# Two attention layers on one core: the P·V sum of a second half copied out by two engines, and a score bank lent to the maxima

## The chip, the cores and the metric

The kernel runs on one core of a Trainium2 chip. The metric is the device time of one execution in microseconds (us). TensorE (PE) multiplies matrices, and its results land in eight banks of 128 partitions by 512 float32 columns; VectorE (DVE) and ScalarE (ACT) read those banks. GpSimd (POOL) works on the other memory alone, and SyncE (SP) issues most transfers.

## The reference

A block is applied twice: a Fourier mixing layer and then an attention layer, each behind a layer norm and added to its input.

```python
x = A_x                                   # 1 x 2048 x 512
x = x + _A_ref(_layernorm(x), ...)        # Re(DFT_seq(DFT_hidden(x))), as matrix products
x = x + _B_ref(_layernorm(x), wq, wk, wv, wo)
x = x + _A_ref(_layernorm(x), ...)
x = x + _B_ref(_layernorm(x), wq, wk, wv, wo)

def _B_ref(x, wq, wk, wv, wo):            # 32 heads of 16; one key and one value head for all
    q = (x @ wq).reshape(B, S, H, Dh).transpose(0, 2, 1, 3)
    k = x @ wk
    v = x @ wv
    scores = einsum("bhqd,bkd->bhqk", q, k) * Dh ** -0.5
    p = softmax(scores)
    o = einsum("bhqk,bkd->bhqd", p, v)
    return o.transpose(0, 2, 1, 3).reshape(B, S, H * Dh) @ wo
```

All is float32.

## The kernel before, in words

Both layers have the same two phases. Phase A makes the Fourier mix, the queries, keys and values. Phase B, where the change lies, makes the attention.

Phase B goes over 16 tiles of 128 queries (`i`), and over 32 steps in each tile (`s_`): a tile has two halves (`hf`) of 16 heads, and a half has 16 steps, one for each chunk of 128 keys (`c`). One step does this:

- It multiplies the probabilities of two steps ago with the values: `pv`, L1137, four products for four groups of heads, added up over the 16 steps of a half in the one bank `z`. After the sixteenth step the sum is copied out of `z` to a tile `row` (L1146 or L1148); after that the next half may begin in `z`.
- It makes four score products (`score`, L1123) in four banks `x`, which are used in turn, and ScalarE takes the exponential of each (L1125).
- It makes a share of the row maxima that later tiles need. These are score products again, in three banks `y`, from which VectorE takes maxima: two whole ones (`whole`, product L450, maximum by L451) and one in two parts (`part`). The first part's product (L1070, g = 0) is followed by a copy of one element by VectorE (L1072), for which the second part's product (L1070, g = 1) waits; one maximum (L1075) then covers both.

The three kinds are interleaved in a fixed order, written as `"asMssMsb"`: a and b are the two parts, M a whole maximum, s a score. PE is strictly in this order. Where a step has two shares of maxima instead of three, another short table sets the order.

The banks of the maxima are in a list, `o.banks`, and those of the scores in a list `o.x`. A product takes the first bank of its list, and the bank goes to the list's end when its reader has been issued.

In step 17 of each tile but the first (`out_now`) the output projection of the tile before stands ahead of the step's scores: twelve products (L102 to L104) in a bank taken from `o.banks`. ScalarE copies that bank out (L1211), and it goes to the end of `o.banks`. In tiles 1 to 5 the step has two shares of maxima, in tiles 6 to 14 three. In tile 15 the maxima run out after a few steps, and the rest of the phase uses wider banks (`wide`).

The sum of a first half is completed in step 17 too (two steps behind), just ahead of the projection; the sum of a second half in step 1 of the next tile, between ordinary steps. The copies to HBM (`o_store`) and the rest of the output's way have half a tile of time.

Waits between engines are put in by the tile framework from what each instruction reads and writes. The order on each engine is the order in which the code issues.

Of the kernel before, what the change touches and what calls it, by code (L numbers as in the profile page):

```python
# [48 lines left out]
def fnet_mqa_kernel(ctx: ExitStack, tc: tile.TileContext, x_in, ct, dt_, wq, wkv, wo, out):  # L49
    nc = tc.nc  # L50
# [5 lines left out]
    def banks_as(name):  # L56
        if layout:
            layout.pop().close()
        if name:
            layout.append(ExitStack())  # L60
            layout[0].ps = layout[0].enter_context(tc.tile_pool(name=name, bufs=1, space=PSUM, reuse_waits="tile"))
# [4 lines left out]
    def f(ap):  # L66
        return ap.bitcast(F32)

    def slot(k, dtype=F32):
        return sb.tile([P, S], dtype, name=f"slot{k}")  # L70

    def half(k, dtype=F32):
        return sb.tile([P, D], dtype, name=f"row{k}")

    def bank(tag):
        if tag == "w":
            return layout[0].ps.tile([P, 1024], F32, name=tag, bufs=3)
        if tag == "v":
            return layout[0].ps.tile([P, 512], F32, name=tag, bufs=1)
        return (psz if tag == "z" else layout[0].ps).tile([P, 512], F32, name=tag, bufs={"x": 4, "y": 3, "z": 1}[tag])  # L80

    def pair():
        return [bank("x") for _ in range(2)]
# [127 lines left out]
    def make_layer(L, src, mid, dst, last):  # L211
        o = Layer()
# [836 lines left out]
        def side():  # L1049
            return min(ahead[0][3]) if ahead else 0  # L1050

        def more_max():
            whole(side())

        def part_next():
            if parts:
                return *parts.pop(), 1
            for e, (i, pr, kb) in enumerate(todo):
                if i in o.loaded | {0} and kb > 1:
                    parts.append(todo.pop(e))  # L1060
                    return *parts[0], 0
            return None
# [23 lines left out]
        def left(j, lim):  # L1086
            def n(of):
                return sum(u[0] < j or (u[0] == j and u[1] < lim) for u in of)
            return 2 * n(todo) + n(parts) + sum(len(u[3]) for u in ahead if u[0] < j or (u[0] == j and u[1] < lim))

        def share(n):
            slack = min([3 * (at - n) - left(j, lim) for j, lim, at in goals if at > n], default=99)
            if n < NSTEP:
                st["light"] = slack >= EARLY_SPARE and not st.get("light") and n >= 4
            else:
                st["light"] = slack >= SPARE and n % NSTEP == NT + 1
            return 2 if st["light"] else 3

        def done_with(i, pr):
            return all(u[:2] > (i, pr) for u in todo + parts + ahead)  # L1100

        ptiles = {}
        wide = []
# [26 lines left out]
        def pv(i, s_):  # L1130
            hf, c = divmod(s_, NT)
            if c == 0:
                acc[i, hf] = bank("z")
            a = acc[i, hf]
            pt = ptiles.pop((i, s_))
            for j in range(4):
                nc.tensor.matmul(a[32 * j:32 * j + 32, :], v1[:, c, :], pt[:, j, :], start=c == 0, stop=c == NT - 1)  # L1137
            if c == NT - 1:
                oa = half(hf)
                if last and (i, hf) == (NT - 1, 1):  # L1140
                    ob = half(0)[:, :256]
                    nc.scalar.copy(oa[:, :256], a[:, :256])
                    nc.vector.tensor_copy(ob, a[:, 256:])
                    oa = (oa, ob)
                elif wide and hf == 0:
                    nc.vector.tensor_copy(oa, a)  # L1146
                else:
                    nc.scalar.copy(oa, a)  # L1148
                acc[i, hf] = oa

        bt = {}
# [51 lines left out]
        def o_proj(i):  # L1203
            for k in range(NK):
                o_mm(k)
            o_add(i)
# [92 lines left out]
        def phase_b(nxt):  # L1299
            nonlocal woh, wol, osp  # L1300
            o.x = pair() + pair()
            o.banks = [bank("y") for _ in range(3)]
            woh = slot(4, F32R).rearrange("p (k e) -> p k e", k=NK)
            wol = slot(5, F32R).rearrange("p (k e) -> p k e", k=NK)
            def wo_load(j):
                st["wo", j] = half(4 + j)
                nc.sync.dma_start(st["wo", j], wo[:, j, :])

            behind = []
            for n in range(NT * NSTEP):  # L1310
                i, s_ = divmod(n, NSTEP)
                if len(behind) == 2:
                    pv(*behind.pop(0))
                behind.append((i, s_))
                out_now = i > 0 and s_ == NT + 1
                if out_now:
                    o_proj(i - 1)
                n_max = share(n) if todo or parts or ahead else 0
                if n_max == 0 and not wide:
                    banks_as(f"wide{L}")  # L1320
                    o.banks = [bank("v")]
                    wide.extend(bank("w") for _ in range(3))
                at = part_next() if n_max == 3 else None
                if at:
                    for k, v in zip("asMssMsb", (0, 1, 0, 3, 0, 1, 2, 1)):
                        if k == "s":
                            score(i, s_, v)
                        elif k == "M":
                            whole(v)
                        else:  # L1330
                            part(at, v)
                else:
                    g = side()
                    turns = ((g, 0), (1 - g, min(n_max, 2)), (2 + g, 0), (3 - g, n_max - 2))
                    if out_now and n_max == 2:
                        whole(g)
                        turns = ((1 - g, 0), (g, 1), (3 - g, 0), (2 + g, 0))
                    for j, m in turns:
                        score(i, s_, j)
                        for _ in range(m):  # L1340
                            more_max()
                if n in (1, 3):
                    q_half_store(12, 2 + n // 2)
                if i == 0 and 17 <= s_ <= 23 and s_ % 2:
                    q_half_store(14, s_ // 2 - 8)
                if 12 <= n < 16:
                    wo_load(n - 12)
                if n == 25:
                    osp = slot(3, F32R).rearrange("p (a h n) -> p a h n", a=2, h=2)
                if i == 0 and s_ in (16, 18, 20, 22):  # L1350
                    j = s_ // 2 - 8
                    nc.gpsimd.tensor_copy(woh[:, j, :], st["wo", j])
                    nc.gpsimd.tensor_sub(wol[:, j, :], st["wo", j], f(woh[:, j, :]))
                if i > 0:
                    for fn in out_tasks(i - 1).get(s_, ()):
                        fn()
                for j in range(2, NT):
                    if i == (j // 4 if j < 5 else j - 4 if j < 13 else j - 2):
                        at = {2: 0, 3: 12, 4: 6}.get(j, 0)
                        if s_ == at:  # L1360
                            qT_load(j)
                        if s_ == at + 4:
                            o.loaded.add(j)
                for fn in half_tasks(i).get(s_, ()):
                    fn()
                for at, j, p0, np_ in ((NT - AHEAD, i, HALF, HALF), (NSTEP - AHEAD, i + 1, 0, HALF if i >= NT - 3 else NPAIR)):
                    if j in (0, NT - 2, NT - 1) or j == i + 1 < NT:
                        for e in range(2):
                            if s_ == at - 1 + e:
                                assert done_with(j, p0 + np_ // 2 * (e + 1) - 1)  # L1370
                                max_neg_a(j, p0, np_, parts=(e,))
                        if s_ == at + 1:
                            max_neg_b(np_, nc.gpsimd)
                        if s_ == at + 2:
                            max_rows(j, p0, np_)
            if nxt is not None:
                wide.clear()
                banks_as(f"single{L + 1}")
                nxt.a_start()
            for at in behind:  # L1380
                pv(*at)
            if nxt is not None:
                o.banks = []
            return {**out_tasks(NT - 1), 12: [lambda: o_proj(NT - 1)]}
# [67 lines left out]
```

## Time and profile before

| | us |
|---|---|
| median of 3 runs (lowest, highest) | 3451.92 (3450.12, 3452.2) |
| profiled execution | 3454.01 |
| its span (first to last instruction) | 3452.2 |
| PE busy, of the span | 3423.4 (99%) |
| DVE busy | 2655.5 (77%) |
| ACT busy | 2669.4 (77%) |
| POOL busy | 936.8 (27%) |
| copies of P·V sums by ACT (L1148), 61 of 617 ns | 37.6 |
| copies of the projection by ACT (L1211), 28 of 587 ns | 16.4 |

Phase B of the first layer runs from about 620 to 1730 us of the span, that of the second from about 2335 to the end. In the first layer tile 7 begins at about 1110 us and tile 8 at about 1180. A PE share of 99% says little, since the products are pipelined and their ends are modelled; what tells more is the time from the first P·V product of a step to that of the next, which is the step's length.

### The profile page before, as it was taken

How to read it: one execution, taken by the hardware profiler on the slowest of the kernel's cores; microseconds unless marked ns; L12 is line 12 of the kernel's file. 1: busy time of each engine (PE TensorE's matmuls, PEld its weight loads, DVE VectorE, ACT ScalarE, POOL GpSimd, SP SyncE). 2: the span in 40 equal slices, each digit the busy share in tenths (PEclk: the TensorE clock that was granted, in tenths of full speed). 3: DMA queues.
4: the chain of work that ended last, by engine and by line, in shares of the span. 5: the costliest groups of instructions: out<-in, count | busy, mean ns of one | idle time of the engine just before them, and what ended most of it. 6: DMA issues, size and time to landing. Idle time of an engine off the chain costs nothing.

```text
span 3452.2 us, 68576 instructions
## 1 busy us (share of the span) xinstructions
PE 3423.4 (99%) x25532; PEld 2012.5 (58%) x25532; DVE 2655.5 (77%) x5772; ACT 2669.4 (77%) x5248; POOL 936.8 (27%) x1478
## 2 busy tenths in 40 slices
PE   8999999999999999999999999999999999999999
PEld 6888979544444444444378979894444444444443
DVE  6264766899899999999432747668989998999893
ACT  4234644899999999999932256549999999999998
POOL 4255453312222222222312354522111111111111
PEclk9999999999999999999999999999999999999999
DMA  6445252321111110111143352423111111011110
GB/s 189 150 156 190 75 168 84 86 64 33 38 36 51 35 27 24 51 35 27 42 141 116 124 173 101 152 73 91 48 39 36 51 36 38 23 36 39 32 30 26
DMA packets 225555, 255.89 MB, mean 74 GB/s; under 512 B 52896, under 2 KB 175040, under 8 KB 218052
## 3 DMA queue, kind: packets, MB, share of 16 engines
q1 hardware_dynamic: 210932, 234.04, 22.0%
q0 software_dynamic: 14144, 17.33, 1.6%
q8 instruction: 201, 3.29, 0.4%
q14 instruction: 134, 1.10, 0.1%
q10 hardware_dynamic: 144, 0.13, 0.0%
HBM read 187.69 MB, written 65.79 MB: 73 GB/s over the span
## 4 chain that ended last, share of the span: by engine, by line
PE 92%; issue 3%; POOL 2%; ACT 1%; DVE 1%; DMA 0%; DVEq 0%; SPq 0%; ACTq 0%; POOLq 0%
PE z L1137 30%; PE x L1123 13%; PE x L893 11%; PE y L1070 10%; PE y L450 8%; PE y L102 3%; PE y L541 3%; PE y L103 2%; PE y L104 2%; PE x L102 2%; PE x L104 2%; PE x L103 2%; PE z L541 1%; PE w L1115 1%; PE z L289 1%
## 5 line engine op out<-in xcount | busy, mean ns | idle before, releaser
L1125 ACT ACTIVATE slot<-x 128x512 f32<-128x512 f32 x3904 | 1994.7, 609 | 27.2 <-PE x L1123 7.3
L451 DVE TENSOR_REDUCE mxp<-y 128x1 f32<-128x512 f32 x1956 | 1259.9, 685 | 89.9 <-PE x L1123 24.7
L1137 PE MATMUL z<-slot,v 128*32 128x512 f32 x8192 | 1102.6, 605 | 0.0
L1123 PE MATMUL x<-slot,kz 64*128 64x512 f32 x2880 | 805.0, 427 | 0.3 <-DMA slot<-craw 0.2
L1075 DVE TENSOR_REDUCE mxp<-y 128x2 f32<-128x512 f32 x956 | 651.2, 681 | 1.1 <-PE x L1123 1.1
L1070 PEld LDWEIGHTS y<-kz,slot 64*128 64x128 f32 x1408 | 258.5, 184 | 583.7 <-DVE mxp L451 568.4
L450 PE MATMUL y<-kz,slot 64*128 64x512 f32 x1440 | 572.4, 417 | 0.6 <-DVE mxp L451 0.4
L1070 PE MATMUL y<-kz,slot 64*128 64x256 f32 x1408 | 468.2, 333 | 0.3
L1123 PEld LDWEIGHTS x<-slot,kz 64*128 64x128 f32 x2880 | 429.1, 185 | 26.5 <-ACT slot L1125 21.2
L893 PE MATMUL x<-cl,xnh 64*128 64x512 f32 (+1 forms) x1536 | 358.5, 354 | 0.0
L893 PE MATMUL x<-ch,xnl 64*128 64x512 f32 (+1 forms) x1536 | 346.3, 358 | 3.1 <-ACT xnl L652 3.1
L893 PE MATMUL x<-ch,xnh 64*128 64x512 f32 (+1 forms) x1536 | 346.5, 358 | 0.2
L450 PEld LDWEIGHTS y<-kz,slot 64*128 64x128 f32 x1440 | 264.1, 185 | 77.2 <-DVE y L1072 22.1
L1137 PEld LDWEIGHTS z<-slot,v 128*32 128x32 f32 x8192 | 167.2, 108 | 229.0 <-issue 183.5
L893 PEld LDWEIGHTS x<-ch,xnh 64*128 64x128 f32 x1536 | 214.8, 184 | 17.8 <-issue 5.2
L893 PEld LDWEIGHTS x<-ch,xnl 64*128 64x128 f32 x1536 | 213.4, 184 | 19.9 <-issue 6.1
L893 PEld LDWEIGHTS x<-cl,xnh 64*128 64x128 f32 x1536 | 217.1, 185 | 9.3
L1185 POOL TENSOR_TENSOR row<-row,row 128x256 f32<-128x256 f32 x63 | 46.5, 738 | 592.7 <-DMA row<-rd 539.0
L93 ACT CAST ch<-craw 128x512 fp32r<-128x512 f32 x176 | 106.4, 623 | 122.0 <-PE x L104 81.6
L1072 DVE COPY y<-y 1x1 f32<-1x1 f32 x956 | 140.9, 147 | 76.1 <-PE y L1070 72.9
L541 PE MATMUL y<-kz,slot 64*128 64x512 f32 x488 | 189.2, 397 | 2.7 <-DVE mxe L557 2.2
L1213 POOL TENSOR_TENSOR row<-row,row 128x512 f32<-128x512 f32 x30 | 38.4, 1279 | 526.5 <-ACT row L1211 526.5
(241 smaller groups left out, 5571.6 us busy)
## 6 DMA issues: line engine op xcount, KB each, us to landing
craw<-ct_in SPq DMA_DIRECT2D x112, 512.0 KB
slot<-qd SPq DMA_DIRECT2D x44, 1024.0 KB
qd<-row SPq DMA_DIRECT2D x144, 128.0 KB
od<-row SPq DMA_DIRECT2D x252, 64.0 KB
row<-wqd SPq DMA_DIRECT2D x48, 256.0 KB
row<-x_in SPq DMA_DIRECT2D x32, 256.0 KB
mid<-row POOLq DMA_DIRECT2D x32, 256.0 KB, 2.4
craw<-ct_in SPq DMA_DIRECT2D x32, 256.0 KB
```

Of the source, the lines that this page charges most:

```text
L102: nc.tensor.matmul(ps_, ah, bh, start=start, stop=False)
L103: nc.tensor.matmul(ps_, ah, bl, start=False, stop=False)
L450: nc.tensor.matmul(pm, o.qT[i][gs, pr, :], kz[gs, c0:c0 + n], start=True, stop=True)
L451: nc.vector.reduce_max(to, pm, axis=AX.X)
L541: nc.tensor.matmul(pm, o.qT[i][gs, pr, :], k[gs, c0:c0 + 512], start=True, stop=True)
L893: nc.tensor.matmul(z[d], a[gs, s, d * P:(d + 1) * P], b[gs, :], start=first and q < 2 and e == 0, stop=last and q > 1 and e == len(turns) - 1)
L1070: nc.tensor.matmul(pm[:, 256 * g:256 * g + 256], o.qT[i][gs, pr, :], kz[gs, c0:c0 + 256], start=True, stop=True)
L1072: nc.vector.tensor_copy(pm[:1, 256:257], pm[:1, :1])
L1075: nc.vector.reduce_max(partial(i)[:, pr, :, k], pm.rearrange("p (a n) -> p a n", a=2), axis=AX.X)
L1123: nc.tensor.matmul(e, kz[64 * g:64 * g + KR, c * P:(c + 1) * P], o.qT[i][64 * g:64 * g + KR, cp:cp + 4, :], start=True, stop=True)
L1125: nc.scalar.activation(ptiles[i, s_][:, j, :], e, AF.Exp, scale=DH ** -0.5)
L1137: nc.tensor.matmul(a[32 * j:32 * j + 32, :], v1[:, c, :], pt[:, j, :], start=c == 0, stop=c == NT - 1)
```

## The change

Two things change. When the copy out of `z` is one of a second half (or the first half of tile 0, which has no projection behind it), and the wide banks are not yet in use, ScalarE copies the left 256 columns and VectorE the right 256. First halves of the other tiles stay whole on ScalarE. And in step 17 of a tile with three shares of maxima, the bank of the projection, which stands last in `o.banks`, goes to the end of the score banks, and the first of the score banks goes to the end of the maxima's.

```diff
@@ def pv
                 elif wide and hf == 0:
                     nc.vector.tensor_copy(oa, a)
+                elif wide or hf == 0 and i > 0:
+                    nc.scalar.copy(oa, a)
                 else:
-                    nc.scalar.copy(oa, a)
+                    nc.scalar.copy(oa[:, :256], a[:, :256])
+                    nc.vector.tensor_copy(oa[:, 256:], a[:, 256:])
                 acc[i, hf] = oa
@@ def phase_b
                 if out_now:
                     o_proj(i - 1)
                 n_max = share(n) if todo or parts or ahead else 0
+                if out_now and n_max == 3:
+                    o.x.append(o.banks.pop())
+                    o.banks.append(o.x.pop(0))
                 if n_max == 0 and not wide:
```

Below the added lines, line numbers are three or six higher: the copies are L1148 (whole), L1150 (ScalarE's half) and L1151 (VectorE's half), and L1211 becomes L1214. The program holds 33 split copies, 32 of them between steps of phase B (16 in each layer) and one at the end of the first layer's; 28 whole ones by L1148 stay.

VectorE at the start of tile 7 in the first layer, before: `row1` is the tile that takes a sum, `z` the bank of the sum, `y_7939` to `y_7941` the banks of the maxima, `mxp` the maxima.

```order
L1075 TENSOR_REDUCE mxp1_11497<-y_7939 128x2
L1072 COPY y_7940<-y_7940 1x1
L451 TENSOR_REDUCE mxp1_11497<-y_7941 128x1
L451 TENSOR_REDUCE mxp1_11497<-y_7939 128x1
L1075 TENSOR_REDUCE mxp1_11497<-y_7940 128x2
```

The same place on VectorE now:

```order
L1075 TENSOR_REDUCE mxp1_11502<-y_7939 128x2
L1151 COPY row1_13481<-z_13088 128x256
L1072 COPY y_7940<-y_7940 1x1
L451 TENSOR_REDUCE mxp1_11502<-x_7935 128x1
L451 TENSOR_REDUCE mxp1_11502<-y_7939 128x1
L1075 TENSOR_REDUCE mxp1_11502<-y_7940 128x2
```

VectorE's half of the copy stands behind the last maximum of step 0 and ahead of step 1's one-element copy (L1072). In the built program it waits for ScalarE's half to have been done.

PE behind the projection in step 17 of tile 6, before: `x_7935` to `x_7938` are the score banks, and the projection's bank is `y_7941`.

```order
L1070 MATMUL y_7939<-kz_73,xnl_86 128x256
L1123 MATMUL x_7935<-slot0_9538,kz_73 128x512
L450 MATMUL y_7940<-kz_73,xnl_86 128x512
L1123 MATMUL x_7936<-slot0_9538,kz_73 128x512
L1123 MATMUL x_7937<-slot0_9538,kz_73 128x512
L450 MATMUL y_7941<-kz_73,xnl_86 128x512
L1123 MATMUL x_7938<-slot0_9538,kz_73 128x512
L1070 MATMUL y_7939<-kz_73,xnl_86 128x256
L1137 MATMUL z_13081<-slot7_13027,v1_75 32x512 x4
```

The same place on PE now:

```order
L1070 MATMUL y_7939<-kz_73,xnl_86 128x256
L1123 MATMUL x_7936<-slot0_9540,kz_73 128x512
L450 MATMUL y_7940<-kz_73,xnl_86 128x512
L1123 MATMUL x_7937<-slot0_9540,kz_73 128x512
L1123 MATMUL x_7938<-slot0_9540,kz_73 128x512
L450 MATMUL x_7935<-kz_73,xnl_86 128x512
L1123 MATMUL y_7941<-slot0_9540,kz_73 128x512
L1070 MATMUL y_7939<-kz_73,xnl_86 128x256
L1137 MATMUL z_13088<-slot7_13034,v1_75 32x512 x4
```

The order of the products is the same. The projection's bank is taken one product later: by the fourth score, where it was taken by the second whole maximum, which now has a bank that was a score's.

## The prediction

> **What bounds the kernel now.** I read the chain of work that ended last, then the busy time of the engines over one stretch of phase B, then the waits of PE's weight loads, and last the order in time around one place of each kind that the change touches.
>
> ```profile
> PE 92%; issue 3%; POOL 2%; ACT 1%; DVE 1%; DMA 0%; DVEq 0%; SPq 0%; ACTq 0%; POOLq 0%
> ```
> ```profile
> 1094.00:1129.00 35.00, 35.00 (x276) 15.42 (x272) 33.73 (x74) 34.67 (x69) 13.97 (x30) 1.00 0.19 55
> ```
> ```profile
> PEld z L1137 <- ACT row L1148: 7.4, 32, 0.3
> PEld y L450 <- ACT row L1211: 6.8, 18, 0.4
> ```
>
> The chain is PE's. But the second row, a stretch around a tile's start (PE, weight loads, VectorE, ScalarE, POOL; then the granted clock, 1.00), shows VectorE busy for 33.73 and ScalarE for 34.67 of 35 us: three engines run side by side, and a microsecond of work moved from one to another may turn up as a wait. The last two rows are the waits that the change aims at: 32 times the next P·V product waits for ScalarE's copy of a sum, and 18 times a maximum's product waits for ScalarE's copy of the projection. Those idle times are of the weight loads, which overlap products, so the price on PE has to be read from PE's own rows. Here are the steps around tile 7's start (start, length, engine; PE's merged groups):
>
> ```profile
> 1108.00 1.06 PE L1137 MATMUL z<-slot,v 128*32 128x512 f32 x8
> ...
> 1110.01 1.06 PE L1137 MATMUL z<-slot,v 128*32 128x512 f32 x8
> ...
> 1111.97 0.49 PE L1123 MATMUL x<-slot,kz 64*128 64x512 f32 x1
> ...
> 1112.39 1.06 PE L1137 MATMUL z<-slot,v 128*32 128x512 f32 x8
> ...
> 1114.40 1.07 PE L1137 MATMUL z<-slot,v 128*32 128x512 f32 x8
> ...
> 1116.52 1.06 PE L1137 MATMUL z<-slot,v 128*32 128x512 f32 x8
> ```
>
> The sum of the second half is complete behind the products at 1108.00. From there the steps last 2.01, 2.38, 2.01 and 2.12 us; 2.01 and 2.12 are the ordinary pair, and 2.38 is the cost of the copy: 0.37 above the shorter step. The engines beside it:
>
> ```profile
> 1109.33 0.62 ACT L1148 COPY row<-z 128x512 f32<-128x512 f32 x1
> ```
> ```profile
> 1108.73 0.68 DVE L1075 TENSOR_REDUCE mxp<-y 128x2 f32<-128x512 f32 x1
> 1109.41 0.15 DVE L1072 COPY y<-y 1x1 f32<-1x1 f32 x1
> 1109.65 1.29 DVE L451 TENSOR_REDUCE mxp<-y 128x1 f32<-128x512 f32 x2
> 1110.86 0.68 DVE L1075 TENSOR_REDUCE mxp<-y 128x2 f32<-128x512 f32 x1
> 1111.45 0.14 DVE L1072 COPY y<-y 1x1 f32<-1x1 f32 x1
> ```
> ```profile
> 1109.46 0.18 PEld L450 LDWEIGHTS y<-kz,xnl 64*128 64x128 f32 x1
> ...
> 1109.62 0.18 PEld L1070 LDWEIGHTS y<-kz,xnl 64*128 64x128 f32 x1
> ...
> 1111.97 0.18 PEld L1123 LDWEIGHTS x<-slot,kz 64*128 64x128 f32 x1 [0.19 <-ACT slot L1125]
> ...
> 1115.98 0.18 PEld L450 LDWEIGHTS y<-kz,xnl 64*128 64x128 f32 x1 [0.17 <-DVE y L1072]
> ```
>
> ScalarE's copy pushes its exponentials back, and the fourth score at 1111.97 waits for its bank: that is the long step. VectorE's one-element copy (L1072) ends at 1109.41 + 0.15 = 1109.56, and the weight load of the step's last maximum product comes 0.06 later, at 1109.62: whatever delays L1072 delays the last product of the step, and the next P·V products stand behind it. The second whole maximum's load decides between the ordinary lengths: 1.46 behind the step's start (1109.46 less 1108.00) the step lasts 2.01, and 1.58 behind it (1115.98 less 1114.40), waiting for VectorE, 2.12.
>
> **The split copy.** It takes 256 columns from ScalarE and gives them to VectorE, at the head of a queue in which L1072, three maxima and, through L1072, PE's next P·V products wait. The halves do not run side by side: VectorE's waits for ScalarE's. The only split copy that the trace holds, at the kernel's end, does the same; beside its rows, what follows what on VectorE without a wait, and what a late load of that last product costs:
>
> ```profile
> 3443.77 0.37 ACT L1142 COPY row<-z 128x256 f32<-128x256 f32 x1 [1.15 <-PE z L1137]
> ```
> ```profile
> 3444.17 0.42 DVE L1143 COPY row<-z 128x256 f32<-128x256 f32 x1 [21.77 <-ACT row L1142]
> ```
> ```profile
> 734.92 0.14 DVE L1072 COPY y<-y 1x1 f32<-1x1 f32 x1
> 734.98 1.27 DVE L451 TENSOR_REDUCE mxp<-y 128x1 f32<-128x512 f32 x2
> ```
> ```profile
> 735.11 0.18 PEld L1070 LDWEIGHTS y<-kz,xnl 64*128 64x128 f32 x1
> ```
> ```profile
> 735.42 1.06 PE L1137 MATMUL z<-slot,v 128*32 128x512 f32 x8
> ```
>
> VectorE's half, 0.42 us, began at 3444.17, 0.03 behind the end of ScalarE's (3443.77 + 0.37), though VectorE had been idle for 21.77 us. The Trainium skill ("PSUM — Partial Sum Buffer", section "PSUM bank collisions raise a hardware error") says why: two engines must not be in one bank's same quadrant at once, reads against reads included, so such accesses are put in order; the row agrees.
>
> Put in at tile 7's start: ScalarE's half begins at 1109.33, behind its exponentials, and takes 0.37, and 0.03 more behind other work (0.62 in the row above, against the 0.59 of the copy at 1145.40, below): 1109.73. VectorE's half runs from 1109.76 to 1110.18. L1072 starts 0.09 before its forerunner's end (1110.86 + 0.68 = 1111.54 against 1111.45), so from 1110.09 to 1110.24, where it ended at 1109.56. The last product's load follows at 1110.30, and the P·V products 0.31 behind that (735.42 less 735.11): 1110.61, where they began at 1110.01. That is 0.60 late.
>
> The next step wins some back. ScalarE is 0.22 earlier (0.59 less 0.37) and PE 0.60 later, so the fourth score no longer waits. What may wait is the second whole maximum, for VectorE: from L1072 at 1110.09 it is 0.06 to the first maximum (734.92 to 734.98), 1.21 for two (1109.65 to 1110.86), 0.68 for the third and 0.06 to the load: 1112.10, or 1.49 behind the step's start. Just above 1.46, that is a step of 2.04. So the second next P·V products begin at 1110.61 + 2.04 = 1112.65 instead of 1112.39: 0.26 lost, 32 times, 8.3 us. The ends: the whole 0.37 vanishes and nothing takes its place (-11.8 us), or the 0.60 stays and the next step is still 2.38 (+19.2 us).
>
> The 33rd split copy stands at the end of the first layer's attention, with no maximum behind it; 0.25 us at most (0.37 + 0.03 + 0.42 less 0.59, 0.23), counted as nothing. The transfers of a second half's sum are issued by SP once both halves are there, so about 0.2 us later, and the loads queued behind them on SP with them. Their cover is half a tile: GpSimd's scaling, the next reader, waits for transfers for 539 us in all, so nothing of it reaches PE.
>
> ```profile
> POOL row L1185 <- DMA row<-rd: 539.0, 30, 25.6
> ```
>
> **The banks exchanged.** Nothing is added; the 18 waits of a maximum for the projection's copy go, and the step's fourth score waits in its place, one product later. Step 17 of tile 7, a tile with three shares, on PE, its loads and ScalarE:
>
> ```profile
> 1146.05 0.49 PE L1123 MATMUL x<-slot,kz 64*128 64x512 f32 x1
> ...
> 1146.59 1.07 PE L1137 MATMUL z<-slot,v 128*32 128x512 f32 x8
> ```
> ```profile
> 1146.04 0.18 PEld L450 LDWEIGHTS y<-kz,slot 64*128 64x128 f32 x1 [0.38 <-ACT row L1211]
> ```
> ```profile
> 1145.40 0.59 ACT L1211 COPY row<-y 128x512 f32<-128x512 f32 x1 [2.12 <-issue]
> ```
>
> The copy ends at 1145.99 in both orders, since it stands ahead of the step's exponentials. Before, the maximum and the fourth score started together, at 1146.04 and 1146.05, and the P·V products came at 1146.59. Now the maximum goes ahead in a bank whose exponential was done before the projection, and the score starts at 1146.05; from a score held up by ScalarE to the P·V products it is 0.42 (1111.97 to 1112.39): 1146.47. The gain is 0.12, 18 times, 2.2 us; at the least nothing, at the most the wait of 6.8 us.
>
> **The sum.** +8.3 - 2.2 = +6.1 us, on the profiled execution 3454.01 + 6.1 = 3460.1; that execution is 2.1 us above the median of the runs shown, and on the median, 3451.92, it is 3458.0. That is 0.18%, at the edge of the 0.2% (6.9 us) that I take as the least a measurement of this kernel can tell from no change.
>
> **The rivals.**
>
> *The halves overlap, faster.* If VectorE's half ran as soon as VectorE is free, at 1108.73 + 0.59 = 1109.32, it would end at 1109.74, L1072 at 1109.80, and the P·V products would begin at 1109.86 + 0.31 = 1110.17; with a next step of 2.04 the loss of 0.26 becomes a gain of 0.18, 32 times: -5.8 - 2.2 = -8.0, 3443.9 us. For it: ScalarE and VectorE would each read another part. Against it: the row at 3444.17. The Trainium skill (the same page, section "Specifications (TRN2)") has the two engines read at full bandwidth in parallel as long as no bank is shared; here one is, so by the page too this is unlikely.
>
> *VectorE's maxima stay late, slower.* The step after the copy is only 2.04 if the first maximum follows L1072 by 0.06. In the rows at tile 7's start it follows by 0.24 (1109.41 to 1109.65), there because its product was not done. If the gap were 0.22 behind a split copy too, the second maximum's load would come at 1.65, 0.07 behind the 1.58 of a step of 2.12, and the step would last 2.19: 0.41 lost each, 13.1 - 2.2 = +10.9, 3462.8 us. Against it: the product is long done when L1072 is late. It decides early: with 0.03 us more for each copy than I reckon, the kernel is measurably slower.
>
> *The exchange is worth its whole wait.* If the fourth score came late at no cost to the step, 18 waits of 0.38 go: 8.3 - 6.8 = +1.5, 3453.4 us. Against it: the score is still ahead of the P·V products, in PE's strict order.
>
> **How the numbers follow.** The forecast gets 0.45, split about evenly by the bound (its spread, 3455 to 3461, lies on both sides of 3458.8): 0.23 no change, 0.22 slower. VectorE late: 0.20, slower. The whole wait saved: 0.13, no change. The halves overlapping, or another way of losing less, as VectorE's share of the stretch (33.73 of 35) leaves it some room: 0.18, faster. The rest, 0.04, is no change by errors that cancel. Together 0.18 faster, 0.40 no change, 0.42 slower. The range from 3444 to 3466 takes in the overlap and the late maxima, and leaves out the far ends of the two unknown prices.
>
> **What would show it.** In the profile after: VectorE's half of the copy idle until ScalarE's half, at 32 places; the P·V products behind a split copy some 2.6 us after the ones before (2.01 here), and those after them 2.04 later (2.38 here), with no wait of the fourth score for ScalarE. In step 17 of tiles 6 to 14 no maximum waits for the projection's copy, 18 scores do, and that step is 0.12 shorter. The prediction is wrong if VectorE's half starts before ScalarE's ends, or if the step behind a split copy stays above 2.1.

## The result, and the profile after

| | before | after |
|---|---|---|
| median (lowest, highest), 22 runs each | 3451.36 (3449.64, 3453.89) | 3458.05 (3455.82, 3460.08) |
| profiled execution | 3454.01 | 3455.93 |
| its span | 3452.2 | 3454.2 |

The ratio of the times is 1.0019, with a 95% interval from 1.0013 to 1.0024. The changed kernel is 6.7 us slower; the forecast was 6.1 us slower and 3458.0 us. The loss is real, since its interval excludes 1, though by size it lies at the 0.2% that the forecast took as the limit of what can be told.

The two profiled executions differ by only 2.0 us. Most of the rest is not in the change but in how each execution started the attention. First P·V products of the first layer, before and then after (start, length), each with the row of the stretch between them, whose third figure from the end is PE's granted clock, in shares of full speed:

```profile
625.45 1.93 PE L1137 MATMUL z<-slot,v 128*32 128x512 f32 x8
628.75 1.06 PE L1137 MATMUL z<-slot,v 128*32 128x512 f32 x8
```
```profile
625.45:628.75 3.30, 3.30 (x18) 1.39 (x16) 1.73 (x4) 1.85 (x5) 0.00 (x0) 0.57 0.62 161
```
```profile
624.14 1.06 PE L1137 MATMUL z<-slot,v 128*32 128x512 f32 x8
626.16 1.07 PE L1137 MATMUL z<-slot,v 128*32 128x512 f32 x8
```
```profile
624.14:626.16 2.02, 2.02 (x19) 0.96 (x17) 1.79 (x5) 1.97 (x5) 0.00 (x0) 1.00 0.73 207
```

The profiled execution of before began them 1.31 us later and had a first step of 3.30 instead of 2.02 us: 2.6 us that the change does not touch, since no sum is complete there (in the second layer another 0.85, first steps of 2.87 and 2.02). Together that is 3.4 of the 4.7 us by which the two differences disagree.

The long first step goes with a lower clock: over it PE was granted 0.57 of full speed before, and 1.00 after (in the second layer 0.68 and 1.00). All first steps of both layers in the eleven profiles of this study fall in line: twelve lasted 2.00 to 2.03 us at a clock of 1.00, ten lasted 2.87 to 3.30 at 0.57 to 0.69. It belongs to the execution and not to the kernel, as far as one profile of each can tell: the four profiled executions without such a stretch are 1.5 to 2.1 us shorter than the median of their own kernel's runs, and the three with one in each layer are 2.1 to 2.9 longer. So a profile tells here how long a step is, and the medians what the kernel costs, with a microsecond or two of this in them.

The page's chain, and from the waits of PE's weight loads the two that answer to those shown before (us in total, times, longest):

```profile
PE 87%; ACT 5%; issue 3%; DVE 2%; POOL 2%; DMA 1%; SPq 0%; ACTq 0%; DVEq 0%; POOLq 0%
```
```profile
PEld y L1070 <- DVE y L1072: 19.2, 32, 0.6
...
PEld x L1123 <- ACT slot L1125: 12.2, 23, 0.8
```

Of ScalarE's copy of the projection (L1214), those who waited for it (us, times):

```profile
  PEld x L1123: 3.7, 14
...
  PEld y L1123: 1.0, 4
```

The wait of the P·V products for ScalarE's copy (7.4 us, 32 times) and that of the maxima for the projection's copy (6.8 us, 18 times) are gone from the list. At 32 places the second part's load (L1070) now waits 0.60 us for VectorE's one-element copy; the scores' waits for an exponential fell from 25.9 us in 88 places to 12.2 in 23; and 14 + 4 scores wait for the projection. ScalarE and VectorE, which had 1% of the chain each, now have 5% and 2%.

The same places in order of time, at the start of tile 7 in the first layer: PE, its loads, VectorE, ScalarE.

```profile
1107.29 1.06 PE L1137 MATMUL z<-slot,v 128*32 128x512 f32 x8
...
1109.93 1.06 PE L1137 MATMUL z<-slot,v 128*32 128x512 f32 x8
...
1111.95 1.06 PE L1137 MATMUL z<-slot,v 128*32 128x512 f32 x8
```
```profile
1109.62 0.18 PEld L1070 LDWEIGHTS y<-kz,xnl 64*128 64x128 f32 x1 [0.60 <-DVE y L1072]
...
1111.40 0.18 PEld L450 LDWEIGHTS y<-kz,xnl 64*128 64x128 f32 x1
```
```profile
1108.04 0.69 DVE L1075 TENSOR_REDUCE mxp<-y 128x2 f32<-128x512 f32 x1
1109.08 0.42 DVE L1151 COPY row<-z 128x256 f32<-128x256 f32 x1 [0.35 <-ACT row L1150]
1109.42 0.14 DVE L1072 COPY y<-y 1x1 f32<-1x1 f32 x1
1109.48 0.67 DVE L451 TENSOR_REDUCE mxp<-x 128x1 f32<-128x512 f32 x1
```
```profile
1108.64 0.40 ACT L1150 COPY row<-z 128x256 f32<-128x256 f32 x1
```

VectorE is free at 1108.04 + 0.69 = 1108.73 and stands idle for 0.35 us until ScalarE's half ends at 1109.04. Its own half ends at 1109.50, L1072 at 1109.56, the load comes at 1109.62 and the P·V products at 1109.93: a step of 2.64 us, followed by one of 2.02. Before they were 2.01 and 2.38.

Step 17 of tile 7, PE and its loads, with ScalarE's copy of the projection:

```profile
1140.89 1.06 PE L1137 MATMUL z<-slot,v 128*32 128x512 f32 x8
...
1146.06 1.07 PE L1137 MATMUL z<-slot,v 128*32 128x512 f32 x8
```
```profile
1145.18 0.18 PEld L450 LDWEIGHTS x<-kz,slot 64*128 64x128 f32 x1
1145.62 0.18 PEld L1123 LDWEIGHTS x<-slot,kz 64*128 64x128 f32 x1 [0.26 <-ACT row L1214]
```
```profile
1144.98 0.59 ACT L1214 COPY row<-x 128x512 f32<-128x512 f32 x1 [2.05 <-issue]
```

The maximum's load no longer waits (1145.18); the fourth score's does, 0.05 behind the copy's end at 1145.57. The step lasts 5.17 us, where it lasted 5.28 in this tile before (1146.59, in the prediction's rows, less 1141.31):

```profile
1141.31 1.07 PE L1137 MATMUL z<-slot,v 128*32 128x512 f32 x8
```

### The profile page after: what moved, and what is told of

The parts are those of the page before. It is cut to its first block, busy times and chain, and to the rows that moved or that the text cites. A ratio compares the mean times of both kernels' runs of the same rounds, so it can differ in the third digit from the quotient of the medians.

```text
span 3454.2 us, 68643 instructions
## 1 busy us (share of the span) xinstructions
PE 3418.1 (99%) x25532; PEld 2019.8 (58%) x25532; DVE 2664.4 (77%) x5805; ACT 2667.5 (77%) x5248; POOL 936.7 (27%) x1478
## 4 chain that ended last, share of the span: by engine, by line
PE 87%; ACT 5%; issue 3%; DVE 2%; POOL 2%; DMA 1%; SPq 0%; ACTq 0%; DVEq 0%; POOLq 0%
PE z L1137 28%; PE x L893 11%; PE x L1123 10%; PE y L1070 8%; PE y L450 6%; ACT slot L1125 3%; PE x L102 3%; PE y L541 3%; PE x L104 3%; PE x L103 3%; PE y L102 2%; PE y L103 2%; PE y L104 2%; PE x L1070 2%; PE y L1123 1%
## 5 line engine op out<-in xcount | busy, mean ns | idle before, releaser
L1125 ACT ACTIVATE slot<-x 128x512 f32<-128x512 f32 x3410 | 1792.9, 605 | 30.6 <-PE x L1123 13.3
L451 DVE TENSOR_REDUCE mxp<-y 128x1 f32<-128x512 f32 x1618 | 1054.4, 684 | 79.0 <-PE x L1123 23.9
L1123 PE MATMUL x<-slot,kz 64*128 64x512 f32 x2514 | 733.4, 425 | 0.3 <-DMA slot<-craw 0.2
L1075 DVE TENSOR_REDUCE mxp<-y 128x2 f32<-128x512 f32 x802 | 546.1, 681 | 1.3 <-PE x L1123 1.3
L1070 PEld LDWEIGHTS y<-kz,slot 64*128 64x128 f32 x1128 | 206.8, 183 | 477.4 <-DVE mxp L451 452.7
L450 PE MATMUL y<-kz,slot 64*128 64x512 f32 x1132 | 451.5, 416 | 0.6 <-DVE mxp L451 0.4
L1123 PEld LDWEIGHTS x<-slot,kz 64*128 64x128 f32 x2514 | 381.1, 184 | 18.0 <-ACT slot L1125 11.0
L1070 PE MATMUL y<-kz,slot 64*128 64x256 f32 x1128 | 376.2, 334 | 6.4 <-DVE y L1072 6.0
L1125 ACT ACTIVATE slot<-y 128x512 f32<-128x512 f32 x494 | 298.8, 605 | 3.7 <-PE y L1123 1.8
L450 PEld LDWEIGHTS y<-kz,slot 64*128 64x128 f32 x1132 | 206.8, 185 | 60.0 <-DVE mxp L1075 9.4
L451 DVE TENSOR_REDUCE mxp<-x 128x1 f32<-128x512 f32 x338 | 231.3, 684 | 8.5
L541 PE MATMUL y<-kz,slot 64*128 64x512 f32 x488 | 189.2, 397 | 2.7 <-DVE mxe L557 2.2
```

Of the source, the lines that this page charges most:

```text
L450: nc.tensor.matmul(pm, o.qT[i][gs, pr, :], kz[gs, c0:c0 + n], start=True, stop=True)
L451: nc.vector.reduce_max(to, pm, axis=AX.X)
L541: nc.tensor.matmul(pm, o.qT[i][gs, pr, :], k[gs, c0:c0 + 512], start=True, stop=True)
L1070: nc.tensor.matmul(pm[:, 256 * g:256 * g + 256], o.qT[i][gs, pr, :], kz[gs, c0:c0 + 256], start=True, stop=True)
L1075: nc.vector.reduce_max(partial(i)[:, pr, :, k], pm.rearrange("p (a n) -> p a n", a=2), axis=AX.X)
L1123: nc.tensor.matmul(e, kz[64 * g:64 * g + KR, c * P:(c + 1) * P], o.qT[i][64 * g:64 * g + KR, cp:cp + 4, :], start=True, stop=True)
```

## The experiments

Each edit is made to the kernel before. The branch that leaves the first halves of tiles 1 to 15 whole, as in the change, belongs to every edit of the sum's copy and is not shown again. Lengths of steps are means over the first layer's tiles 6 to 14, taken from the starts of P·V products as above; "copy step" is the one in which a second half's sum is copied out, "next step" the one behind it, "projection step" step 17.

| | median, us | ratio to before [95%] | copy step | next step | projection step |
|---|---|---|---|---|---|
| before | 3451.4 | | 2.02 | 2.39 | 5.29 |
| after | 3458.05 | 1.0019 [1.0013, 1.0024] | 2.65 | 2.02 | 5.17 |
| split alone | 3460.28 | 1.0024 [1.0014, 1.0034] | 2.64 | 2.02 | 5.30 |
| exchange alone | 3449.25 | 0.9994 [0.9985, 1.0002] | 2.02 | 2.39 | 5.17 |
| VectorE's half alone | 3444.89 | 0.9980 [0.9971, 0.9989] | 2.18 | 2.02 | 5.29 |
| whole copy by VectorE | 3453.23 | 1.0004 [0.9996, 1.0013] | 2.45 | 2.02 | 5.29 |
| split 384 and 128 | 3458.37 | 1.0020 [1.0011, 1.0029] | 2.62 | 2.02 | 5.29 |
| VectorE's half behind L1072 | 3457.95 | 1.0016 [1.0007, 1.0025] | 2.25 | 2.34 | 5.29 |
| maximum last | 3449.88 | 0.9996 [0.9987, 1.0004] | 2.02 | 2.39 | 5.16 |
| half projection copy, exchange | 3445.66 | 0.9982 [0.9973, 0.9991] | 2.03 | 2.39 | 4.96 |
| half projection copy, maximum last | 3448.53 | 0.9991 [0.9982, 1.0000] | 2.03 | 2.39 | 5.13 |

The runs of before beside them had medians of 3451.66 (first four experiments), 3451.37 (next three) and 3451.50 (last two); differences below are taken against these.

### The two parts by themselves

The change's first edit alone, and its second alone:

```diff
-                    nc.scalar.copy(oa, a)
+                    nc.scalar.copy(oa[:, :256], a[:, :256])
+                    nc.vector.tensor_copy(oa[:, 256:], a[:, 256:])
```
```diff
+                if out_now and n_max == 3:
+                    o.x.append(o.banks.pop())
+                    o.banks.append(o.x.pop(0))
```

> Only the split copies; no bank is exchanged. My theory (VectorE's half waits for ScalarE's half, and the one-element copy L1072 and with it the next P*V products wait behind both): 32 places at 0.25 us, +8 us against the kernel before, so about 3459.5; behind each split copy a step of 2.6 us and then one of 2.0. Rival (the exchange is worth nothing, and the split is the whole of the change): +6.7, the same as the changed kernel.

> Only the bank exchange in step 17 of tiles 6 to 14; the copies of the sums stay whole on ScalarE. My theory: 18 steps shorter by 0.12 us, -2.1 us against the kernel before, about 3449.3; the step with the projection 5.17 instead of 5.28, and the wait for the projection's copy moved to the fourth score. Rival (the wait only changes its owner): 0. Rival (the whole wait is saved): -5.8 to -6.8.

The split alone costs 8.6 us, the exchange alone changes the median by -2.4 us; together that is +6.2, where +6.7 was measured for both. The parts add up. The steps agree: the split's two steps last 2.64 + 2.02 instead of 2.02 + 2.39, 0.25 us more (in the second layer too), and behind them the ordinary pair only changes places, 2.11 and 2.01 where it was 2.01 and 2.12. Whole tiles are 0.30 us longer in the first layer and 0.27 in the second, and the projection step is 0.12 shorter, 18 times 2.2 us. From the steps alone the whole change would cost 32 times 0.25 less 2.2, 5.8 us, where the interval of the medians goes from 4.5 to 8.3. The interval of the exchange alone reaches just past 1, so the time by itself does not tell it from no change; the step does.

### Is it the wait between the halves?

Here ScalarE's half is left out (GpSimd writes ones in the left half of those sums, which is therefore not computed), so that VectorE's half has nothing to wait for but the product:

```diff
-                    nc.scalar.copy(oa, a)
+                    nc.gpsimd.memset(oa[:, :256], 1.0)
+                    nc.vector.tensor_copy(oa[:, 256:], a[:, 256:])
```

> VectorE copies its 256 columns at the same places, but ScalarE copies nothing there: the left half of those sums is left out, and GpSimd writes ones in its place. So VectorE's half has no other engine to wait for in the bank, and its own work is that of the split. My theory (the cost of the split is the wait for ScalarE's half): the copy starts as soon as VectorE is free, the next P*V products come 2.2 us after the ones before and the next ones 2.0 after that; 0.18 gained at 32 places, -5.8 us against the kernel before, about 3445.5. Rival (VectorE has no room, its 0.34 us of work is the cost, whatever it waits for): the 2.6 us step stays, and the result lies at +5 to +8.

It is 6.8 us faster than before. VectorE and the load behind it, at the start of tile 7:

```profile
1105.76 0.68 DVE L1075 TENSOR_REDUCE mxp<-y 128x2 f32<-128x512 f32 x1
1106.36 0.41 DVE L1151 COPY row<-z 128x256 f32<-128x256 f32 x1
1106.69 0.14 DVE L1072 COPY y<-y 1x1 f32<-1x1 f32 x1
```
```profile
1105.03 1.07 PE L1137 MATMUL z<-slot,v 128*32 128x512 f32 x8
...
1107.20 1.06 PE L1137 MATMUL z<-slot,v 128*32 128x512 f32 x8
```
```profile
1106.89 0.18 PEld L1070 LDWEIGHTS y<-kz,xnl 64*128 64x128 f32 x1
```

The same copy of the same 256 columns starts without a gap behind the maximum. L1072 begins 1.66 us behind the step's start (1106.69 less 1105.03), in the kernel after 2.13 (1109.42 less 1107.29), and the step lasts 2.17 instead of 2.64: 0.47 us on VectorE turn into 0.47 us on PE. Between this and the split alone lie 15.4 us (3460.28 less 3444.89), 0.48 for each of 32 places. ScalarE is relieved of its half as well here, but the next step lasts 2.02 with it and without it, so that is not what counts. That the halves stand in a row is the whole loss, and more than that.

### Is the split at fault, or VectorE's taking part?

> VectorE copies all 512 columns at the 32 places and ScalarE none. Twice the split's work on VectorE, but one instruction, and no wait for ScalarE. My theory (two fixed parts and a handover in a row are the cost): from 1109.32 to 1110.01 in the times of tile 7's start, L1072 0.17 earlier than with the split; the next P*V products 2.43 behind the ones before, the next ones 2.04 after; 0.09 lost at 32 places, +2.9 us, about 3454.3. Rival (VectorE's work is the cost): the split's +8 and 0.27 more at each place, +17.

The edit gives all 512 columns of those sums to VectorE (`nc.vector.tensor_copy(oa, a)`). VectorE, and the load:

```profile
1108.87 0.68 DVE L1150 COPY row<-z 128x512 f32<-128x512 f32 x1
1109.47 0.14 DVE L1072 COPY y<-y 1x1 f32<-1x1 f32 x1
```
```profile
1109.67 0.18 PEld L1070 LDWEIGHTS y<-kz,xnl 64*128 64x128 f32 x1 [0.40 <-DVE y L1072]
```
```profile
1107.54 1.06 PE L1137 MATMUL z<-slot,v 128*32 128x512 f32 x8
...
1109.98 1.06 PE L1137 MATMUL z<-slot,v 128*32 128x512 f32 x8
```

Twice the columns delay VectorE less than half of them: L1072 starts 1.93 behind the step's start (1109.47 less 1107.54), where the split had 2.13. In VectorE's own queue, without a handover, the whole copy costs 1.6 us on the median, within the interval of no change, where the split costs 8.6. The expected 2.9 lies in the same interval; the two steps are 0.06 longer than before, which is 1.9 us for 32 places.

Next, another place for the cut: ScalarE 384 columns, VectorE 128 (in the split edit, 384 for 256).

> Split copies alone, as in the first experiment, but ScalarE takes 384 columns and VectorE 128. My theory (what counts is when the second of two copies in a row ends): ScalarE's part 0.11 longer, VectorE's 0.13 shorter, the end 0.02 to 0.03 earlier; about +7.5 us against the kernel before, near the +8.6 of the even split. Rival (VectorE's work is the cost): half of it is gone, +4 us.

```profile
1109.38 0.51 ACT L1150 COPY row<-z 128x384 f32<-128x384 f32 x1
```
```profile
1109.92 0.29 DVE L1151 COPY row<-z 128x128 f32<-128x128 f32 x1 [0.46 <-ACT row L1150]
```

+7.0 us, hardly better than the even cut. VectorE's copy is 0.13 shorter and starts 0.11 later, since the two stand in a row: 0.51 + 0.29 = 0.80 here, 0.40 + 0.42 = 0.82 with the even cut. From VectorE's 0.29, 0.42 and 0.68 for 128, 256 and 512 columns, 128 columns cost 0.13 and each copy some 0.16 besides; ScalarE's 0.40, 0.51 and 0.62 for 256, 384 and 512 give 0.11 and some 0.18. A split pays a fixed part on each engine.

### Does it help to let L1072 go first?

The even split, but VectorE's half is put by until the next step's one-element copy (and, where a step has none, to its end):

```diff
+                    nc.scalar.copy(oa[:, :256], a[:, :256])
+                    held_back.append((oa[:, 256:], a[:, 256:]))
...
                             part(at, v)
+                            copy_back()
```

`copy_back()` issues VectorE's copy if one is held back.

> Split copies alone, with VectorE's half issued behind the next step's one-element copy (L1072) instead of ahead of it. My theory: L1072 is on time, so the last product of the step is too; the next P*V products then wait for the bank itself, 2.24 behind the ones before instead of 2.64, and the maxima run 0.45 late, so that the following step is 2.35 instead of 2.04; 0.20 lost at 32 places, +6.4 us. Rival (the place on VectorE's queue is what costs): near 0.

+6.6 us: the copy step falls to 2.25, but the next one is back at 2.34. In this kernel's numbering L1133 is VectorE's half and L1142 the P·V product:

```profile
1109.48 0.16 PEld L1142 LDWEIGHTS z<-slot,v 128*32 128x32 f32 x8 [0.43 <-DVE row L1133]
...
1111.27 0.18 PEld L450 LDWEIGHTS y<-kz,xnl 64*128 64x128 f32 x1 [0.30 <-DVE y L1072]
```

The P·V products now wait for the half itself, since the sum's bank must be empty, and the second whole maximum of the next step waits 0.30 us for VectorE's one-element copy. In both places that were tried for VectorE's half, PE waits for it.

### Can the projection step lose the whole wait?

Without the exchange, in the projection's step only, the second whole maximum goes behind the fourth score and the second part:

```diff
-                    for k, v in zip("asMssMsb", ...
+                    for k, v in zip("asMssbsM" if out_now else "asMssMsb", ...
```

> Neither the split nor the exchange: in the 18 steps with the projection and three shares, the second whole maximum's product goes to the end of the step, and takes the projection's bank there. My theory: no product of PE waits for the projection's copy any more; that step is 4.96 instead of 5.28, and as the maximum is then late on VectorE, the next one may be 2.12 instead of 2.01; -3.8 to -5.8 us against the kernel before, about 3446.5. Rival (the stall comes back whole in the next step): 0.

This expectation failed: -1.5 us, and a step of 5.16, the same as with the exchange. Loads of tile 7:

```profile
1145.16 0.18 PEld L1070 LDWEIGHTS y<-kz,slot 64*128 64x128 f32 x1 [0.35 <-issue]
...
1145.79 0.18 PEld L1070 LDWEIGHTS y<-kz,slot 64*128 64x128 f32 x1 [0.22 <-DVE y L1072]
1145.80 0.18 PEld L1123 LDWEIGHTS x<-slot,kz 64*128 64x128 f32 x1
1145.95 0.18 PEld L450 LDWEIGHTS y<-kz,slot 64*128 64x128 f32 x1
```

The second part, one place further forward, now waits for the one-element copy, 0.63 us behind the first part's load, and the score and the maximum stand behind it. But the maximum's load is also just 0.04 behind the end of ScalarE's copy (1145.32 + 0.59, from its row). To tell the two apart, ScalarE's copy was halved in both orders; the left half of the projection's addend is then not computed:

```diff
-                nc.scalar.copy(raw, bt["po"])
+                nc.gpsimd.memset(raw[:, :256], 1.0)
+                nc.scalar.copy(raw[:, 256:], bt["po"][:, 256:])
```

> The banks exchanged as in the change, the sums copied whole by ScalarE, and ScalarE copies only the right 256 columns of the projection's bank (the left half of that addend is not computed, ones stand for it). In the run with the exchange alone the fourth score's load came 0.05 behind the copy's end and 0.79 behind the first part's load (1145.54 less 1144.75), and the P.V products 0.43 behind it: a step of 5.17. The half copy ends some 0.2 earlier. If the copy alone sets the step, the load moves to about 0.6 and the step is 4.96 to 5.00, 18 times: 3.1 to 3.8 us less than with the exchange alone, about 3446. If the step has another bound close by (VectorE's one-element copy, behind which the second part's load can't come before 0.63), the step stays above 5.1 and the time above 3448.

> The order with the whole maximum last in the projection's step, without the exchange, and the same half copy of the projection (its left half is not computed). With the whole copy this order gave steps of 5.16, where two waits end together: the second part's load for VectorE's one-element copy (to 1145.79), and the last maximum's load at 1145.95, 0.04 behind the end of ScalarE's copy. If ScalarE's copy held the maximum, the step falls to about 5.0, as in the other run of this pair, and the time to about 3446.5. If the one-element copy holds it, with the score and the maximum queued behind the second part, the step stays at 5.12 to 5.16 and the time within 1 us of 3449.5.

With the exchange the step falls to 4.96, with the other order only to 5.13. Loads of the first, then of the second:

```profile
1143.98 0.18 PEld L1070 LDWEIGHTS y<-kz,slot 64*128 64x128 f32 x1 [0.35 <-issue]
...
1144.56 0.18 PEld L1123 LDWEIGHTS x<-slot,kz 64*128 64x128 f32 x1
1144.61 0.18 PEld L1070 LDWEIGHTS y<-kz,slot 64*128 64x128 f32 x1
```
```profile
1142.57 0.18 PEld L1070 LDWEIGHTS y<-kz,slot 64*128 64x128 f32 x1 [0.22 <-DVE y L1072]
1142.57 0.18 PEld L1123 LDWEIGHTS x<-slot,kz 64*128 64x128 f32 x1
1142.67 0.19 PEld L450 LDWEIGHTS y<-kz,slot 64*128 64x128 f32 x1
```

With the banks exchanged it is ScalarE's copy that holds the step: 0.22 us less of it is 0.21 us less of step. The step behind gives 0.12 of that back (2.13 instead of 2.01); the tile as a whole is 0.15 us shorter than with the exchange alone (69.45 against 69.60). With the maximum last the one-element copy holds it, wait and all, and the shorter copy brings 0.03. So the order with the maximum last does move the wait for ScalarE to the step's end, where it is nearly over, but a wait for VectorE of about the same length stands beside it. With the half copy the maximum's load comes 0.10 behind the second part's (1142.67 less 1142.57), with the whole copy 0.16 (1145.95 less 1145.79): the two waits let it go within 0.06 us of each other, and taking away the one makes the step 0.03 shorter.

## Why the prediction was right

**The split copy.** Every link came out within 0.03 us of what was reckoned. VectorE's half waits for ScalarE's at 32 places:

```profile
L1151 DVE COPY row<-z x33: 416/425/425, 656.6 to 3382.2; 128x256 f32<-128x256 f32 x33
...
  ACT row L1150: 11.6, 32
```

From the start of the P·V products, the prediction had ScalarE's half from 1.33 to 1.73, VectorE's from 1.76 to 2.18, the load at 2.30 and the next products at 2.61; tile 7 has 1.35 to 1.75, 1.79 to 2.21, 2.33 and 2.64. The next step was put at 2.04 and lasts 2.02, because the second maximum's load comes 1.47 behind its start (1111.40 less 1109.93), not 1.49. Late by 0.63, 0.36 won back: 0.27 in this tile against the forecast 0.26 (0.25 in the mean), and 8.6 us on the median of the run with the split alone against 8.3. The rule of the Trainium skill ("PSUM — Partial Sum Buffer", section "PSUM bank collisions raise a hardware error") that two engines' accesses to one bank and the same quadrant of 32 partitions are put in order fits what the traces show, with either cut. The rows show that the built program waits; what the banks would do without the wait, no run here shows, nor what a cut by partitions instead of columns would have brought.

**The 33rd copy and the transfers** were costed at nothing, and no cost of theirs shows. The 33rd copy lies between the first layer's last P·V products and the second layer's first: from the start of the former's last merged group to the latter it is 612.15 us before (1727.80 to 2339.95) and 611.79 after (1728.07 to 2339.86). For the transfers there is only the sum: the 32 places account for 8.0 to 8.6 us (0.25 to 0.27 each), and the interval of the split alone, 4.8 to 11.7 us, could hide a small rest.

**The exchange.** The wait moved to 18 scores, and the step is 0.12 shorter, as worked out from 0.42 between a held-up score and the P·V products: measured 1146.06 less 1145.62, 0.44. The bounds (0 to 6.8 us) were wide because the trace of before did not show which product could bear the wait. The halved copy shows now that with this order the step bears it: 0.22 us less of copy made the step 0.21 shorter, and 0.15 of that stayed in the tile.

**The rivals.** *The halves overlap* is refuted by the wait rows; its price was about right, though: with the wait taken away VectorE's half brought 6.8 us, where the rival's copy term was 5.8. ScalarE's half was left out for that, so two halves read side by side were not run. *VectorE's maxima stay late* is refuted by L1072 at 1109.42 and the maximum at 1109.48, 0.06 behind, and by a next step of 2.02 instead of 2.19. *The exchange is worth its whole wait* (0.38 a step) is refuted by 5.17 instead of 4.91.

**What was off.** On the profiled execution the forecast was 3460.1, and that execution took 3455.93: the start of the attention, shown above, differed between the two profiled executions by 3.4 us, more than half of the forecast change. The forecast on the median depends on it less. That the median came out within 0.1 us of 3458.0 is partly luck: the change was 6.7 us, not 6.1, and the median of before in the longer series was 0.6 lower than the one first shown.

The exchange alone (3449.25) has a lower median than either kernel. Its gain over before is 0.06% with an interval that reaches past 1, so it rests on the step's 0.12 us, not on the time.

## What to carry to other kernels

Splitting a copy between two engines shortens it only if both may read at once; from one bank they went in a row here, because the built program waits, with two fixed parts and a handover, and a copy of 0.62 us (ScalarE's, whole, at this place before) took 0.86 from the first half's start to the second's end (1108.64 to 1109.50). Before moving work to another engine, find the small instruction in that engine's queue for which the critical engine waits (here a copy of one element), and count from there: here it came 0.72 us later (2.13 us behind the step's start instead of 1.41) and the step became 0.63 longer, while what the relieved engine gave back in the next step was 0.36. And when a wait is to be taken away, work out the next one behind it: with the maximum moved last it ended 0.06 us earlier, and with the half copied later the copy step's 0.39 us (2.64 to 2.25) came back as 0.32 in the next step (2.02 to 2.34).

## What was not expected of the hardware

That a late one-element copy delays PE was reckoned from one late load in the trace before (0.31 us from the load to the P·V products). It held, without loss, for all three delays tried: load times of 1.86, 2.13 and 2.33 us behind the step's start (VectorE's half alone, whole copy by VectorE, split) gave steps of 2.17, 2.44 and 2.64, each 0.31 more. And the first attention step of a layer took 2.0 us in some executions and 2.9 to 3.3 in others, at a granted clock of 1.00 or of 0.57 to 0.69, with no change in the program that touches it. It falls both ways in the two layers of one execution too: with VectorE's half alone it lasted 2.01 us in the first layer and 2.88 in the second, with the whole copy by VectorE 3.11 and 2.01. What lowers the clock there stays open.
